# Branch hint, first score unit by halves, and a split last output piece in a soft-capped attention and token/channel mixer

## The chip, the core and the metric

The kernel runs on one core of one Trainium2 chip. The metric is the device time of one execution in microseconds (us). The kernel before took 591.39 us (median of 3 runs, 590.9 to 591.47).

## The reference, cut to what matters

```python
batch, heads, seq, head_dim = 4, 12, 448, 64          # attention
scores = tanh((q @ k.T) / sqrt(64) / cap) * cap       # soft cap
attn = exp(scores - max); attn /= attn.sum(-1) + 1e-9
x = heads_side_by_side(attn @ v)                      # 4 x 448 x 768

h = relu(x.T @ w_tok1) @ w_tok2                       # token mixing, 448 -> 256 -> 448
u = x + h.T
out = u + relu(u @ w_ch1) @ w_ch2                     # channel mixing, 768 -> 1536 -> 768
```

All inputs and the output are float32.

## The kernel before, in words

The work has three parts. The **attention** works on pairs of heads (two heads of 64 rows fill the 128 partitions) and on blocks of 128 keys: a score unit (`qk_unit`, line 349) is a matmul of a key block with all 448 queries for both heads. ScalarE then takes its tanh (`tanh_unit`, line 384) and its exp (line 394), and a `pv` unit multiplies the result with v. The first score units use plain float32 operands straight from the load (line 363); each such matmul call is issued to TensorE as two weight loads and two matmuls. Later units use operands split in a high and a low part. **Token mixing** is filled into the gaps of the attention. The **channel mixing** runs in six groups of 256 hidden channels; for each group and each of the 4 batches a `ch1` stage (line 834, 36 matmuls of 448 columns) makes the hidden values and a `ch2` stage (line 864, six output pieces of 6 matmuls) multiplies them back. `add_out` (line 883) lets VectorE add each piece to u and, in the last group, sends the sum to the output with one DMA per piece from SP's queue. The very last piece is added and sent in two halves of 224 columns, the first from SP's queue and the second from ScalarE's.

The first instructions are written by hand. `load_pair` (line 305) brings q and k of the first head pair in three DMAs: q on SP's queue (line 308), the first 128 keys on ScalarE's queue (line 309), and, after the small `cap` (line 310), the other keys on SP's queue (line 311). Behind them SP issues the second pair, v, the third pair and v twice more (lines 313 and 334). Two warm-up matmuls (line 742) keep TensorE busy meanwhile. After that a planner written in the kernel (`Plan`, line 87) simulates the engines with fixed costs and decides the order in which jobs are emitted; its costs are not touched by the change.

Near the end there is a **branch**. The fast way of computing holds only where `cap` is at most 40, so `big` is loaded from `mag` (line 1024) and compared (line 1025). All engines take this branch. The arm that runs here holds the last `ch1`, the `ch2` that was pending and the last `ch2` (lines 1028 to 1030). The other arm, `general()` (line 996), recomputes everything slowly and is never run with these inputs; with `preferred_fallthrough_block=False` its instructions lie directly behind the branch in the program, and the arm that runs lies behind them, about 9,970 TensorE instructions further on. `general()` calls `ch2` too (line 1021), with the same last piece. A branch hint for this branch is asked for at line 958, after `ch1` of the last group's third batch; the call names no engine.

Of the kernel before, what the change touches and what calls it, by code (L numbers as in the profile page):

```python
# [11 lines left out]
AF = mybir.ActivationFunctionType  # L12
ALU = mybir.AluOpType
PSUM = bass.MemoryType.PSUM

P = 128
B, H, S, D = 4, 12, 448, 64
C = H * D
NC = C // P
# [8 lines left out]
GF = 2  # L28
NG = FF // (GF * P)
# [4 lines left out]
FREE = 40.0  # L34
EPS = 1e-9
WARM = 2
WHOLE = S + NF * P
TERMS = ((0, 0), (1, 0), (0, 1))

SWITCH = {("pv", "qk"): 200, ("qk", "bg"): 195, ("bg", "pv"): 147, ("qk", "pv"): 143, ("bg", "qk"): 199}  # L40
DRAIN = 250
# [45 lines left out]
class Plan:  # L87
# [27 lines left out]
    def job(self, engine, cost, took, emit, *deps, slack=0.0, key=None):  # L115
        deps += (self.pe if self.at is None else self.at,)
        j = Job(cost, took if engine in ("sp", "pool") else took + SIGNAL, emit, deps, slack)
        self.jobs[engine].append(j)
        if key is not None:
            self.done[key] = j  # L120
        return j
# [48 lines left out]
def tile_softcap_mixer(ctx, tc, qk, v, cap, w1, w2, wc1, wc2, out):  # L170
    nc = tc.nc
# [11 lines left out]
    tsc = const.tile([P, 1], F32, name="tsc")  # L183
# [3 lines left out]
    u = [const.tile([P, NC, S], F32, name=f"u{b}") for b in range(B)]  # L187
# [11 lines left out]
    plan = Plan()  # L199
    job, done = plan.job, plan.done  # L200
# [6 lines left out]
    def room(n):  # L207
        return rings[n].room
# [85 lines left out]
    def half(i, j):  # L294
        return slice((i ^ j) * D, ((i ^ j) + 1) * D)
# [4 lines left out]
    def fine(b, p):  # L300
        return (b, p) >= FINE
# [3 lines left out]
    def load_pair(b, p):  # L305
        raw = pi.tile([P, 2, S], F32, tag="qkraw", name="qkraw", bufs=3)
        if b == 0 and p == 0:
            nc.sync.dma_start(raw[:, 0], qk[b, p, :, 0])
            nc.scalar.dma_start(raw[:, 1, :P], qk[b, p, :, 1, :P])
            nc.sync.dma_start(cap_sb, cap)  # L310
            nc.sync.dma_start(raw[:, 1, P:], qk[b, p, :, 1, P:])
        else:
            nc.sync.dma_start(raw, qk[b, p])
        raws[b, p] = raw
        holds["raw", b, p] = rings["raw"].take(NK)
        if not fine(b, p):
            return
        hi, lo = (pi.tile([P, WHOLE], F32R, tag=f"qk{x}", name=f"qk{x}", bufs=3) for x in ("hi", "lo"))
        parts[b, p] = hi, lo
        both = raw.rearrange("p x s -> p (x s)")[:, :WHOLE]  # L320
        near_first = len(parted) < INSIDE
        parted.append((b, p))

        def high():
            nc.gpsimd.dma_start(hi, both if near_first else qk[b, p].rearrange("p x s -> p (x s)")[:, :WHOLE])

        def low():
            nc.vector.tensor_tensor(lo, both, hi, op=ALU.subtract)

        job("pool", 560, 4 * P * WHOLE, high, *([("raw", b, p)] if near_first else []), slack=1500.0, key=("hi", b, p))  # L330
        job("dve", 1020, 1040, low, ("hi", b, p), ("raw", b, p), slack=LATER, key=("lo", b, p))
# [5 lines left out]
    def fetch(b, p):  # L337
        job("sp", 373, 8 * P * S, lambda: load_pair(b, p), room("raw"), slack=1500.0, key=("raw", b, p))
# [10 lines left out]
    def qk_unit(b, p, c):  # L349
        ps = ps_a.tile([P, 2, 512], F32, tag="a", name="ps_qk")  # L350
        hold = rings["a"].take(1)
        if c < NF and fine(b, p):
            two = parts[b, p]
            ks = slice(S + c * P, S + (c + 1) * P)
            for n, (x, y) in enumerate(TERMS):
                for j in range(2):
                    r = slice(j * D, (j + 1) * D)
                    nc.tensor.matmul(ps[:, j, :S], two[x][r, ks], two[y][r, :S], start=(n == 0), stop=(n == 2))  # L358
        elif c < NF:
            raw = raws[b, p]  # L360
            for j in range(2):
                r = slice(j * D, (j + 1) * D)
                nc.tensor.matmul(ps[:, j, :S], raw[r, 1, c * P:(c + 1) * P], raw[r, 0], start=True, stop=True)
        else:
            for i in range(2):
                raw = raws[b, p + i]
                for j in range(2):
                    r = slice(j * D, (j + 1) * D)
                    nc.tensor.matmul(
                        ps[half(i, j), i, :S], raw[r, 1, NF * P:S], raw[r, 0], start=True, stop=True  # L370
                    )
        t = plan.spend(612 if fine(b, p) and c < NF else 750, "qk")
        for i in range(2 if c == NF else 1):
            h = holds["raw", b, p + i]
            h.read(t)
            if len(h.by) == NK:
                raws.pop((b, p + i))
                parts.pop((b, p + i), None)
                n = pairs.index((b, p + i)) + 3
                if n < len(pairs):  # L380
                    fetch(*pairs[n])
        tanh = job("act", 891, 1009, lambda: tanh_unit(b, p, c, ps, hold, tanh), t + DRAIN, room("e"))

    def tanh_unit(b, p, c, ps, hold, tanh):
        e = pe.tile([P, 2, S], F32, tag="e", name="e", bufs=8)
        nc.scalar.activation(e, ps[:, :, :S], AF.Tanh, scale=tsc)  # L386
        hold.read(tanh)
        es[b, p, c] = e
        holds["e", b, p, c] = rings["e"].take(3 if c == NF else 2)
        job("act", 932, 1042, lambda: exp_unit(b, p, c), tanh.end - 190, slack=300.0, key=("exp", b, p, c))  # L390
# [349 lines left out]
    zeros = nc.const_aps.tensor(0.0, [P, HALF], F32)  # L740
    for _ in range(WARM):
        nc.tensor.matmul(idle[:, :HALF], zeros[:, :P], zeros, start=True, stop=True)
# [50 lines left out]
    while t < steps_in:  # L793
        n = 2 if PAIRED[0] <= t < PAIRED[1] else 1
# [33 lines left out]
    def await_key(key):  # L828
        await_time(lambda: plan.ready([key]))

    def await_weights(name, g, i):
        await_key(((name, g), i // DU * DU))
# [30 lines left out]

    def ch2(w, b, x, last, g=0):
        await_key(("g", g, b))
        for cc in range(NC):
            clear(lambda: rings["b"].room() is None and rings["c"].room() is None)
            n, tag = min((free_at(tag), tag) for tag in ("b", "c"))
            plan.pe = max(plan.pe, n)
            ps = (ps_b if tag == "b" else ps_c).tile([P, 512], F32, tag=tag, name="ps_o")  # L870
            hold = rings[tag].take(1)
            cs = slice(cc * P, (cc + 1) * P)
            n = 0
            for i in range(GF):
                await_weights("wc2", g, i * C + cc * P)
                for wi, gi in ((0, 0), (1, 0), (0, 1)):
                    nc.tensor.matmul(ps[:, :S], w[:, wi, i, cs], x[:, gi, i, :], start=(n == 0), stop=(n == 3 * GF - 1))  # L877
                    n += 1
            plan.spend(6 * 204)
            hold.read(job("dve", 530, 612, lambda cc=cc, ps=ps: add_out(b, cc, ps, last), plan.pe + DRAIN))  # L880
            fill()

    def add_out(b, cc, ps, last):
        end = last and b == B - 1 and cc == NC - 1
        for i, q in enumerate((nc.sync, nc.scalar) if end else (nc.sync,)):
            r = slice(i * S // 2, (i + 1) * S // 2) if end else slice(0, S)
            nc.vector.tensor_tensor(u[b][:, cc, r], u[b][:, cc, r], ps[:, r], op=ALU.add)  # L887
            if last:
                q.dma_start(out[b, :, cc, r], u[b][:, cc, r])

    def free_at(tag):
        t = rings[tag].room()
        return float("inf") if t is None else t
# [12 lines left out]
    def clear(more):  # L906
        while more():
            if not chunk():
                rest()
# [31 lines left out]
    w = w0  # L941
    for g in range(NG):
        if g + 1 < NG:
            nxt, steps = group_weights(
                g + 1, ([("tok",)], [("tok",)]) if g == 0 else ((), [("ch2", g - 1)]), slack=60000.0
            )
            for step in steps:
                step()
        if g == 0:
            pend = first_group(w)  # L950
            w = nxt
            continue
        for b in range(B):
            if g == NG - 1 and b == B - 1:
                break
            gt = ch1(w[0], b, g)
            if g == NG - 1 and b == B - 2:
                tc.mark_branch_hint_location("big", hint="LikelyTaken")
            ch2(*pend)
            if pend[1] == B - 1:  # L960
                done["ch2", pend[4]] = plan.pe
            pend = (w[1], b, gt, g == NG - 1, g)
        w = nxt
# [117 lines left out]
```

## Time and profile before

| | us |
|---|---|
| median of 3 runs | 591.39 |
| the profiled execution's own time | 589.29 |
| span of its instructions | 587.5 |
| TensorE busy (matmuls) | 579.7 |
| ScalarE busy | 255.5 |
| VectorE busy | 405.0 |

A row of a timeline has start, length, engine, line, operation, output and inputs, how many instructions it merges, and in brackets the idle time of the engine just before with what ended it. PE is TensorE's matmuls, PEld its weight loads; a q behind an engine's name (SPq, PEldq) is work of its instruction sequencer: DMA issues, branches, semaphores. "issue" is idle time in which the engine waited for nothing that the profile shows.

### The profile page before, as it was taken

Reading aid. Unit: us, or ns where it says so; the run is one execution under the profiler, and the core shown is the slowest. Engines: PE = TensorE matmul, PEld = TensorE weight load, DVE = VectorE, ACT = ScalarE, POOL = GpSimd, SP = SyncE. Lnnn points to the kernel's source line nnn. Section 1 sums busy time; section 2 is a strip of 40 time slices with the busy share of each in tenths; the row PEclk is TensorE's granted clock in tenths of the full one; section 3 lists DMA queues with packets and bytes.
Section 4 is the critical chain, followed back from the end, with each engine's and each line's share of the span. In section 5 each row is a group of like instructions: output and inputs, shape, how many; then the busy total and the mean of one; then the engine's idle time right before and its main releaser. Section 6 shows DMA issues by size and latency. Waiting matters only on the chain.

```text
span 587.5 us, 7994 instructions
## 1 busy us (share of the span) xinstructions
PE 579.7 (99%) x3102; PEld 449.5 (77%) x3102; DVE 405.0 (69%) x681; ACT 255.5 (43%) x330; POOL 9.2 (2%) x23
## 2 busy tenths in 40 slices
PE   8999999999999999999999999999999999999997
PEld 2233445545647899999999999999999999999986
DVE  2999999999999987479895568356835653333324
ACT  7999999899796433142430212021202110000000
POOL 0000100001000000000000000000000000000000
PEclk9999999999999999999999999999999999999999
DMA  7544684667521140003342032003200200000224
GB/s 243 183 148 137 193 260 161 207 222 227 180 80 38 38 134 6 1 1 98 117 144 73 0 108 79 29 0 108 77 32 1 71 1 0 1 0 32 94 84 172
DMA packets 26779, 55.51 MB, mean 94 GB/s; under 512 B 7024, under 2 KB 16752, under 8 KB 26736
## 3 DMA queue, kind: packets, MB, share of 16 engines
q1 hardware_dynamic: 24288, 48.37, 25.6%
q0 software_dynamic: 2160, 6.39, 3.9%
q8 instruction: 26, 0.43, 0.3%
q10 hardware_dynamic: 288, 0.18, 0.1%
q14 instruction: 17, 0.14, 0.1%
HBM read 47.97 MB, written 5.59 MB: 91 GB/s over the span
## 4 chain that ended last, share of the span: by engine, by line
PE 63%; DMA 1%; DVE 1%; issue 1%; SPq 0%; ACT 0%; DVEq 0%
PE ps_o L877 30%; PE ps_g L845 28%; PE ps_u L615 2%; PE ps_h L592 2%; DMA rs<-sums 1%; PE ps_t L564 1%; DMA rb<-rs 0%; DVE uhl L716 0%; DVE u L621 0%; DVE g L858 0%; DVE wz L246 0%; DVE wc L260 0%; SPq L544 0%; ACT uhl L713 0%; DVE u L887 0%
## 5 line engine op out<-in xcount | busy, mean ns | idle before, releaser
L877 PE MATMUL ps_o<-g,wc 128*128 128x448 f32 x864 | 181.7, 367 | 0.0
L877 PEld LDWEIGHTS ps_o<-g,wc 128*128 128x128 f32 x864 | 161.8, 188 | 14.4
L845 PE MATMUL ps_g<-uhl,wc 128*128 128x448 f32 x648 | 137.6, 367 | 0.0
L845 PEld LDWEIGHTS ps_g<-uhl,wc 128*128 128x128 f32 x648 | 121.1, 188 | 10.5
L887 DVE TENSOR_TENSOR u<-u,ps_o 128x448 f32<-128x448 f32 (+1 forms) x145 | 87.5, 615 | 45.3 <-PE ps_o L877 45.0
L386 ACT ACTIVATE e<-ps_qk,tsc 128x896 f32<-128x896 f32 x84 | 81.4, 1026 | 8.2 <-PE ps_qk L358 3.5
L394 ACT ACTIVATE e<-e,near 128x896 f32<-128x896 f32 x84 | 84.7, 1064 | 0.0
L855 ACT ACTIVATE g<-ps_g 128x896 fp32r<-128x896 f32 x24 | 22.1, 920 | 140.9 <-PE ps_g L845 140.8
L858 DVE SCALAR_TENSOR_TENSOR g<-ps_g,g 128x896 fp32r<-128x896 f32 x24 | 26.1, 1089 | 74.7 <-ACT g L855 74.7
L434 PE MATMUL ps_pv<-e,vn 128*64 128x448 f32 x288 | 60.5, 549 | 0.9 <-ACT e L394 0.9
L256 ACT ACTIVATE wc<-wz 128x512 fp32r<-128x512 f32 x36 | 22.8, 633 | 82.2 <-PE ps_g L845 36.0
L845 PE MATMUL ps_g<-last_u,wc 128*128 128x448 f32 x216 | 45.8, 368 | 1.2 <-PE ps_o L877 0.7
L845 PEld LDWEIGHTS ps_g<-last_u,wc 128*128 128x128 f32 x216 | 40.5, 188 | 5.7 <-issue 1.7
L434 PEld LDWEIGHTS ps_pv<-e,vn 128*64 128x64 f32 x288 | 18.0, 136 | 34.7 <-issue 24.2
L233 ACT ACTIVATE wz<-wraw 128x512 f32<-128x512 f32 x36 | 24.0, 670 | 37.8 <-DVE wc L260 17.4
L260 DVE TENSOR_TENSOR wc<-wz,wc 128x512 fp32r<-128x512 f32 x36 | 24.8, 688 | 21.2 <-ACT wc L256 19.9
L592 PE MATMUL ps_h<-wc,last_u 128*128 128x384 f32 x176 | 33.0, 336 | 0.0
L615 PE MATMUL ps_u<-last_u,wc 128*128 128x448 f32 x144 | 32.9, 371 | 0.0
L592 PEld LDWEIGHTS ps_h<-wc,last_u 128*128 128x128 f32 x176 | 30.8, 188 | 1.0 <-issue 0.6
L473 DVE TENSOR_TENSOR acc<-acc,e 64x448 f32<-64x448 f32 x48 | 29.7, 619 | 1.4
L615 PEld LDWEIGHTS ps_u<-last_u,wc 128*128 128x128 f32 x144 | 26.4, 188 | 5.2 <-issue 1.6
L456 DVE TENSOR_TENSOR acc<-e 128x896 f32<-128x896 f32 x24 | 26.0, 1084 | 6.1 <-ACT e L394 5.8
(59 smaller groups left out, 466.1 us busy)
## 6 DMA issues: line engine op xcount, KB each, us to landing
wraw<-in_wc SPq DMA_DIRECT2D x36, 512.0 KB, 3.5
qkraw<-in_qk SPq DMA_DIRECT2D x23, 448.0 KB, 4.0
vn<-in_v SPq DMA_DIRECT2D x24, 224.0 KB, 3.0
rb<-rs SPq DMA_DIRECT2D x48, 112.0 KB, 3.0
out_t<-u SPq DMA_DIRECT2D x23, 224.0 KB, 1.9
qkhi<-in_qk POOLq DMA_DIRECT2D x12, 416.0 KB, 4.0
qkhi<-qkraw POOLq DMA_DIRECT2D x3, 416.0 KB, 3.3
wraw<-in_w SPq DMA_DIRECT2D x2, 512.0 KB, 5.7
```

The costliest lines, as they stand in the source:

```text
L260: nc.vector.tensor_tensor(lo, bits(held["z"]), hi, op=ALU.subtract)
L386: nc.scalar.activation(e, ps[:, :, :S], AF.Tanh, scale=tsc)
L394: nc.scalar.activation(e, e, AF.Exp, scale=near)
L434: nc.tensor.matmul(o, vn[x % 3][:, j * NF + c], es[b, p, c][:, j], start=first, stop=last)
L456: nc.vector.tensor_tensor(accs[b, q][0][:, i], es[b, p, 0], es[b, p, 1], op=ALU.add)
L473: nc.vector.tensor_tensor(t, t, es[b, p - i, NF][r, i], op=ALU.add)
L592: nc.tensor.matmul(ps[:, :HALF], w, x, start=(n == 0), stop=(n == len(mm) - 1))
L615: nc.tensor.matmul(ps[:, :S], h1[:, hi, t, cs], w2s[:, wi, t, :], start=(n == 0), stop=(n == 3 * NT - 1))
L845: nc.tensor.matmul(ps[:, i, :S], w[:, wi, cc, fs], uhl[b][:, ui, cc, :], start=(n == 0), stop=(n == 3 * NC - 1))
L858: nc.vector.scalar_tensor_tensor(x[:, 1], ps[:, :, :S], 0.0, x[:, 0], op0=ALU.max, op1=ALU.subtract)
L877: nc.tensor.matmul(ps[:, :S], w[:, wi, i, cs], x[:, gi, i, :], start=(n == 0), stop=(n == 3 * GF - 1))
L887: nc.vector.tensor_tensor(u[b][:, cc, r], u[b][:, cc, r], ps[:, r], op=ALU.add)
```

## The change

The hint is asked for after `ch1` of the last group's first batch instead of the third. The first score unit is computed in two halves of 224 query columns, with q's load split the same way (the second half of q goes behind `cap`, ahead of the rest of k), and its tanh is two instructions. The last output piece is computed as two pieces, columns 0 to 335 and 336 to 447, each with its own six matmuls, its own add and its own DMA; the halves of 224 columns are gone.

```diff
+TAIL = 336
     def load_pair(b, p):
         if b == 0 and p == 0:
-            nc.sync.dma_start(raw[:, 0], qk[b, p, :, 0])
+            nc.sync.dma_start(raw[:, 0, :S // 2], qk[b, p, :, 0, :S // 2])
             nc.scalar.dma_start(raw[:, 1, :P], qk[b, p, :, 1, :P])
             nc.sync.dma_start(cap_sb, cap)
+            nc.sync.dma_start(raw[:, 0, S // 2:], qk[b, p, :, 0, S // 2:])
             nc.sync.dma_start(raw[:, 1, P:], qk[b, p, :, 1, P:])
...
-            for j in range(2):
-                r = slice(j * D, (j + 1) * D)
-                nc.tensor.matmul(ps[:, j, :S], raw[r, 1, c * P:(c + 1) * P], raw[r, 0], start=True, stop=True)
+            for n in columns(b, p, c):
+                for j in range(2):
+                    r = slice(j * D, (j + 1) * D)
+                    nc.tensor.matmul(ps[:, j, n], raw[r, 1, c * P:(c + 1) * P], raw[r, 0, n], start=True, stop=True)
...
+    def columns(b, p, c):
+        return [slice(0, S // 2), slice(S // 2, S)] if b == p == c == 0 else [slice(0, S)]
...
-        nc.scalar.activation(e, ps[:, :, :S], AF.Tanh, scale=tsc)
+        for n in columns(b, p, c):
+            nc.scalar.activation(e[:, :, n], ps[:, :, n], AF.Tanh, scale=tsc)
...
     def ch2(w, b, x, last, g=0):
-        for cc in range(NC):
+        pieces = [(cc, slice(0, S)) for cc in range(NC)]
+        if last and b == B - 1:
+            pieces[-1:] = [(NC - 1, slice(0, TAIL)), (NC - 1, slice(TAIL, S))]
+        for cc, r in pieces:
...
-                    nc.tensor.matmul(ps[:, :S], w[:, wi, i, cs], x[:, gi, i, :], start=(n == 0), stop=(n == 3 * GF - 1))
+                    nc.tensor.matmul(ps[:, r], w[:, wi, i, cs], x[:, gi, i, r], start=(n == 0), stop=(n == 3 * GF - 1))
...
-    def add_out(b, cc, ps, last):
-        end = last and b == B - 1 and cc == NC - 1
-        for i, q in enumerate((nc.sync, nc.scalar) if end else (nc.sync,)):
-            r = slice(i * S // 2, (i + 1) * S // 2) if end else slice(0, S)
-            nc.vector.tensor_tensor(u[b][:, cc, r], u[b][:, cc, r], ps[:, r], op=ALU.add)
-            if last:
-                q.dma_start(out[b, :, cc, r], u[b][:, cc, r])
+    def add_out(b, cc, r, ps, last):
+        nc.vector.tensor_tensor(u[b][:, cc, r], u[b][:, cc, r], ps[:, r], op=ALU.add)
+        if last:
+            (nc.scalar if r.start else nc.sync).dma_start(out[b, :, cc, r], u[b][:, cc, r])
...
             gt = ch1(w[0], b, g)
-            if g == NG - 1 and b == B - 2:
+            if g == NG - 1 and b == 0:
                 tc.mark_branch_hint_location("big", hint="LikelyTaken")
```

## Rows read from the trace of the kernel before

**Rows 1.** Windows: busy us (instructions) of each engine; then granted clock, DMA share, GB/s.
```profile
20.00:40.00 20.00, 20.00 (x114) 5.95 (x112) 19.55 (x35) 20.00 (x24) 0.30 (x1) 1.00 0.57 174
...
454.50:558.20 103.70, 103.70 (x508) 95.10 (x507) 41.62 (x67) 10.24 (x13) 0.00 (x0) 1.00 0.08 29
```
**Rows 2.** Chain that ended last, from 555 us (start, us, what).
```profile
560.45 0.69 issue
...
563.61 0.47 issue
...
569.39 14.74 PE ps_o L877 x72
```
**Rows 3.** The branch's line and the hint's line (duration ns min/median/max, start).
```profile
L1025 PEldq COMPARE_BRANCH  x1: 3732/3732/3732, 557.2 to 557.2; - x1
...
nothing on L958; most used: ['L877', 'L845', 'L434', 'L358', 'L592', 'L615', 'L363', 'L369', 'L564', 'L437', 'L485', 'L887', 'L386', 'L394', 'L215', 'L246', 'L233', 'L473', 'L517', 'L544', 'L554', 'L256', 'L530', 'L1076', 'L889']
```
**Rows 4.** Instruction fetches (packets, MB, share): 454.5 to 558.2, 558.2 to 559.7, 561.6 to 562.9.
```profile
q8 instruction: 4, 0.07, 0.2%
...
q8 instruction: 1, 0.02, 5.6%
...
q8 instruction: 1, 0.02, 5.2%
```
**Rows 5.** Timeline of weight loads behind the branch.
```profile
561.11 2.32 PEld L845 LDWEIGHTS ps_g<-last_u,wc 128*128 128x128 f32 x12 [1.06 <-issue]
564.08 4.93 PEld L845 LDWEIGHTS ps_g<-last_u,wc 128*128 128x128 f32 x24 [0.65 <-issue]
```
**Rows 6.** Line of the first score units (duration ns, first and last start).
```profile
L363 PE MATMUL ps_qk<-qkraw x108: 536/536/809, 3.9 to 61.6; 64*128 64x448 f32 x108
```
**Rows 7.** SP's queue at the start, timeline.
```profile
0.75 0.40 SPq L308 DMA_DIRECT2D qkraw<-in_qk  x1
...
1.68 0.43 SPq L311 DMA_DIRECT2D qkraw<-in_qk  x1
```
**Rows 8.** DMA issues at the start (KB each, us from issue to landing).
```profile
qkraw<-in_qk SPq DMA_DIRECT2D x1, 224.0 KB, 2.9
qkraw<-in_qk SPq DMA_DIRECT2D x1, 160.0 KB, 3.4
```
**Rows 9.** Timeline of weight loads and of ScalarE at the first units.
```profile
3.87 0.47 PEld L363 LDWEIGHTS ps_qk<-qkraw 64*128 64x128 f32 x4 [1.33 <-DMA qkraw<-in_qk]
5.13 0.30 PEld L363 LDWEIGHTS ps_qk<-qkraw 64*128 64x128 f32 x4 [0.80 <-DMA qkraw<-in_qk]
...
5.11 2.10 ACT L386 ACTIVATE e<-ps_qk,tsc 128x896 f32<-128x896 f32 x2 [2.44 <-PE ps_qk L363]
7.11 1.03 ACT L394 ACTIVATE e<-e,near 128x896 f32<-128x896 f32 x1
```
**Rows 10.** Timeline of the last add and the last DMA issue.
```profile
584.15 0.69 DVE L887 TENSOR_TENSOR u<-u,ps_o 128x224 f32<-128x224 f32 x2 [0.61 <-PE ps_o L877]
584.87 0.36 ACTq L889 DMA_DIRECT2D out_t<-u  x1
```
**Rows 11.** Lines with narrower matmuls, and the adds (duration ns min/median/max).
```profile
L592 PE MATMUL ps_h<-wc,last_u x176: 332/334/442, 71.0 to 253.1; 128*128 128x384 f32 x176
...
L564 PE MATMUL ps_t<-ident,u x96: 270/272/332, 42.2 to 242.0; 128*128 128x128 f32 x96
...
L887 DVE TENSOR_TENSOR u<-u,ps_o x145: 380/620/623, 224.3 to 584.5; 128x448 f32<-128x448 f32 x143, 128x224 f32<-128x224 f32 x2
```
**Rows 12.** Chain, longer stretches of those lines (start, us, what).
```profile
218.46 3.82 PE ps_h L592 x22
222.28 0.44 PE ps_t L564 x4
```
**Rows 13.** The output's DMAs, all and the two halves (KB, us to landing).
```profile
out_t<-u SPq DMA_DIRECT2D x23, 224.0 KB, 1.9
...
out_t<-u ACTq DMA_DIRECT2D x1, 112.0 KB, 1.7
```

More of the change, by code (lines that the diff above doesn't have):

```diff
@@ L876, in ch2 @@
                 for wi, gi in ((0, 0), (1, 0), (0, 1)):
-                    nc.tensor.matmul(ps[:, :S], w[:, wi, i, cs], x[:, gi, i, :], start=(n == 0), stop=(n == 3 * GF - 1))
+                    nc.tensor.matmul(ps[:, r], w[:, wi, i, cs], x[:, gi, i, r], start=(n == 0), stop=(n == 3 * GF - 1))
                     n += 1
             plan.spend(6 * 204)
-            hold.read(job("dve", 530, 612, lambda cc=cc, ps=ps: add_out(b, cc, ps, last), plan.pe + DRAIN))
+            hold.read(job("dve", 530, 612, lambda cc=cc, r=r, ps=ps: add_out(b, cc, r, ps, last), plan.pe + DRAIN))
             fill()
-    def add_out(b, cc, ps, last):
-        end = last and b == B - 1 and cc == NC - 1
-        for i, q in enumerate((nc.sync, nc.scalar) if end else (nc.sync,)):
-            r = slice(i * S // 2, (i + 1) * S // 2) if end else slice(0, S)
-            nc.vector.tensor_tensor(u[b][:, cc, r], u[b][:, cc, r], ps[:, r], op=ALU.add)
-            if last:
-                q.dma_start(out[b, :, cc, r], u[b][:, cc, r])
+    def add_out(b, cc, r, ps, last):
+        nc.vector.tensor_tensor(u[b][:, cc, r], u[b][:, cc, r], ps[:, r], op=ALU.add)
+        if last:
+            (nc.scalar if r.start else nc.sync).dma_start(out[b, :, cc, r], u[b][:, cc, r])
     def free_at(tag):
```

## Prediction

> **What bounds the kernel now.** I read the windows first. In the attention ScalarE is the full engine: busy 20.00 of 20.00 us, while TensorE's weight loads fill only 5.95. In the channel mixing it is TensorE: 103.70 of 103.70 us, with ScalarE at 10.24 [rows 1]. So time won or lost at the first tanh reaches the end only through ScalarE's queue, and in the channel mixing every nanosecond that TensorE stands still is paid. The chain that ended last shows where it stands still at the end: 0.69 us at 560.45, directly at the branch, and 0.47 us at 563.61, in the middle of a `ch1` stage whose operands had long been ready. Both are put down to "issue", a wait for nothing that the profile knows. From 564.08 on it runs without a gap, the last 72 matmuls in 14.74 us, 0.205 each [rows 2].
>
> The branch's line explains both. TensorE's sequencer, which runs ahead of the array, begins the branch at 557.2 and spends 3732 ns on it [rows 3]: until 560.97 no further instruction enters TensorE's queue. The array had work until 560.45, so 3.2 us of it are hidden and 0.69 (1.06 for the weight loads) are seen. The instruction fetches say what it waited for. Queue 8 made four fetches between 454.5 and 558.2 [rows 4], while TensorE ran 508 + 507 = 1015 instructions [rows 1]: one fetch per about 256 instructions, about 17 KB each. The next is in 558.2 to 559.7, after the branch had begun: the target was brought in only when the branch asked for it. One more follows in 561.6 to 562.9 [rows 4], and the second gap ends after it. Behind the branch 12 weight loads run, and then the loads stop for 0.65 us [rows 5]. One semaphore wait, 12 loads and 11 matmuls make 24 instructions: **the branch's target lies 24 instructions before the end of its fetched block**, and the next block, asked for only after the jump, comes 0.47 us too late.
>
> **Part 1, the hint, and what it would have to do.** No row of the trace stands on the hint's line [rows 3], though branches, register loads and semaphore waits of all engines are recorded. The call names no engine, and the program of the kernel before holds no hint instruction; the moved call names none either. I take that it adds nothing: 0 us. If it did work, the target would come early and both gaps would go, -1.16; that is rival 2.
>
> **A side effect: where the code comes to lie.** The change lengthens TensorE's program in two places ahead of the branch's target. The first score unit has four matmul calls instead of two; line 363 has 108 matmuls for 27 units of two calls [rows 6], so a call is two loads and two matmuls, and the two new calls are 8 instructions. `general()` lies between branch and target, and its `ch2` is split as well: 6 loads and 6 matmuls more, 12 instructions. The target moves 20 instructions on against the blocks of 256, from 24 before a block's end to 4: a semaphore wait, a load, a matmul, a load. The branch itself moves by 8 and is still not in the target's block, so it waits as before. TensorE then has one matmul instead of 11 to do while the second block is brought. If that block arrives when it does now, at 564.08, ten matmuls at 0.205 come after the gap instead of before it: **+2.05**. Bounds: if the second fetch is set off by reaching the block's end and not by the jump, it starts up to 0.65 us earlier (561.0 instead of about 561.65), +1.4. If coming to the end at once costs a fresh request like the branch's own (it began its fetch about 1 us after 557.2, against about 0.7 between the jump's end and the second), +2.4. The near row is the second fetch as it is, so I take 2.05. Nothing covers it: in this stretch TensorE is the chain.
>
> The Trainium skill ("Runtime: NRT & Kernel Launch", section "Instruction fetch mechanics") says that running over the end of a 16 KiB instruction block is mostly hidden, since the next one is fetched while the current one runs. By that sentence the term of 2.05 would be 0; the trace agrees with it for the straight stages, where no gap is seen, and not behind the branch, where the 0.47 stands. It is rival 1.
>
> **Part 2, the start.** Today q's 224 KB are issued at 0.75 and land 2.9 later, the rest of k is issued at 1.68 and lands 3.4 later, at 5.08 [rows 7, 8]. The first unit's loads start at 3.87 and the second unit's at 5.13, both on a DMA; the two tanhs run from 5.11, 2.10 us together, and the first exp starts at 7.11 [rows 9]. After the change q's second half takes the slot at 1.68, so k's rest is issued at 2.15, 0.47 later, and so is every load that SP issues behind it. The first half tanh comes early, at perhaps 4.6, and ScalarE does both halves before 5.9. But the second tanh waits for the second unit, and that for k's rest, at 5.08 + 0.47 = 5.55. ScalarE's queue is in order, so the early half waits in front of it: the second unit shifts by about **+0.45**. Bounds: the bytes ahead of k's rest are the same as before, so if the transfers themselves were the limit it lands at 5.1 again and the shift is -0.1 (the 2.10 for two tanhs hold about 0.1 of waiting); if the narrower rows of q (896 bytes) move no faster than its full ones did, another 0.35 comes on top, +0.8. ScalarE being full, I let two thirds reach the end: +0.3, range -0.1 to +0.8. The later loads (pair 2, v) are asked for in the same order and needed some microseconds after; their 0.47 is hidden behind the tanhs and exps of the first units.
>
> **Part 3, the end.** Six matmuls of 448 columns take 6 x 0.205 = 1.23 now. For 384 columns 22 take 3.82, 0.174 each, and for 128 columns 4 take 0.44, 0.11 each [rows 11, 12]; between 384 and 448 a column costs 0.48 ns. 336 columns: 0.150, six are 0.90. 112 columns: by that slope 0.042, but the near row is the 128-column one, whose weight loads set the pace: 0.11, six are 0.66. Together 1.56, TensorE ends 0.33 later. The first piece's add (about 0.50) and its DMA lie beside the second piece's matmuls and land first. Then the add of 112 columns: 380 ns at 224 columns and 620 at 448 [rows 11] give 0.26, against 0.69 for today's two halves [rows 10]. The last issue moves by 0.33 + 0.26 - 0.69 = -0.10. The last DMA carries 56 KB instead of 112; 224 KB take 1.9 and 112 take 1.7 [rows 13], so 1.6: -0.1. Sum **-0.2**. Bounds: 112 columns at 0.042 give -0.6; at the full 0.205 each, +0.37.
>
> The Trainium skill ("DMA: Bandwidth & Descriptors", section "Specifications") asks for pieces of at least 512 bytes, and 112 columns are 448 bytes per partition. If that doubles the 0.1 us that I give these 56 KB to move, the estimate for this part is -0.1 instead of -0.2; no row here shows a store that narrow.
>
> **Sum.** 2.05 + 0.3 - 0.2 + 0 = +2.15, say +2.1. The profiled execution took 589.29 (span 587.5 and 1.8 around it), so it would be 591.4; the median of the runs stands 2.1 above it at 591.39, and the same step gives **593.5**.
>
> **Rivals.** (1) *The crossing is hidden, or falls elsewhere.* The block's end does not come 4 instructions behind the target: either the 0.47 had another cause, or the number of semaphore waits in `general()` changes by four or more with the planner's state and the target slips into a fresh block. Then the 2.05 is 0 (or -0.47), and the rest leaves +0.1 (or -0.4): 591.5 (591.0), not slower. It decides from the fourth extra instruction on. For it: the other arm is planned anew after a changed piece; against it: a semaphore wait is added only where an instruction has two things to wait for, and the edits add none of that sort. 0.18. (2) *The hint takes effect.* Issued before TensorE enters the branch's block at about 531 it brings the target in time, both gaps go: -1.16 + 0.1, 590.3. Against it: the line without a row. 0.06. (3) *The longer pause slows the array.* The first matmuls of line 363 took 809 ns against a median of 536 [rows 6]; if after 2.7 us of standing still some ten or fifteen matmuls ran at half pace, 0.2 us each, another 2 to 3 us come on top: 596. For it only that first row; against it, matmuls after the 0.69 us gap ran at full pace. 0.04. My forecast, 0.72, has its own range: 1.4 - 0.1 - 0.4 to 2.4 + 0.7 + 0.2, that is 592.4 to 594.6.
>
> The range over the cases reaches down to rival 1 and leaves out the -0.4 variant's low side, rivals 2 and 3: 591.1 to 594.6. A measurement of this kernel tells about 0.2% (1.2 us) from no change. Slower by more than that: nearly all of the forecast and rival 3, 0.73. Within: rival 1, half of rival 2 and the forecast's low end, 0.22. Faster: the other half of rival 2 and what I do not see, 0.05.
>
> **What would show it.** TensorE's branch at line 1025 still near 3.7 us; two weight loads instead of 12 behind the branch, then an issue gap of 2 us or more, ending about 3 us after the jump; no row on the hint's line. At the start, a first tanh near 4.6 and the second unit's loads near 5.6. At the end, six matmuls at 0.15 and six near 0.11, and the last issue 0.1 us nearer to them. Wrong if the stretch behind the branch shows no longer gap, or if the branch takes well under 3 us.

## The result, and the profile after

The changed kernel takes 595.17 us (median of six runs, 593.5 to 597.63), the kernel before 591.38 in six runs beside them: a ratio of 1.0072, 95% [1.006, 1.0083], or +4.3 us [3.5, 4.9] (the two medians alone differ by 3.8). I had forecast 593.5 (591.1 to 594.6): slower, as it came, but by half as much. The profiled execution of after took 594.71 (span 592.8), 0.5 below its median, while that of before lay 2.1 below its own; so the two spans differ by 5.3 us, and about one of these is no work of the change.

The chain of after that ended last (start, us, what), against [rows 2]:

```profile
561.59 0.69 issue
562.28 0.44 PE ps_g L852
562.73 2.85 issue
565.58 8.92 PE ps_g L852 x35
574.50 15.04 PE ps_o L887 x78
589.53 0.02 issue
589.56 0.27 DVE u L894
```

The line numbers are those of the changed kernel: its line 852 is line 845 of before, 887 is 877, 894 is 887 and 1032 is 1025. The first gap is the one of before, 0.69. The second is 2.85 us instead of 0.47 and stands behind one matmul instead of 11. Then there is something that has no counterpart in before: the 36 matmuls of this `ch1` take 0.44 + 8.92 = 9.36 us, where before took 7.79 (2.47 + 5.32):

```profile
561.14 2.47 PE ps_g L845 x11
564.08 5.32 PE ps_g L845 x25
```

The windows of after say why (length; busy us and instructions of PE, PEld, DVE, ACT, POOL; granted clock; DMA share, GB/s):

```profile
562.00:565.00 3.00, 0.44 (x1) 0.19 (x1) 0.23 (x1) 0.00 (x0) 0.00 (x0) 1.00 0.43 153
565.00:567.00 2.00, 1.42 (x5) 1.30 (x6) 0.00 (x0) 0.00 (x0) 0.00 (x0) 0.80 0.06 18
567.00:569.00 2.00, 2.00 (x7) 1.73 (x7) 0.00 (x0) 0.00 (x0) 0.00 (x0) 0.50 0.00 0
569.00:571.00 2.00, 2.00 (x10) 1.85 (x9) 0.00 (x0) 0.00 (x0) 0.00 (x0) 0.85 0.00 0
571.00:573.00 2.00, 2.00 (x12) 1.85 (x11) 0.00 (x0) 0.00 (x0) 0.00 (x0) 1.00 0.00 0
```

Behind the long pause the granted clock falls to 0.50, the lower of the engine's two levels (1.2 instead of 2.4 GHz), and in those 2 us 7 matmuls run instead of the usual 11 or 12. PE is "busy" 2.00 of 2.00 there: the busy share alone would have hidden it. Before has 1.00 in every one of these windows, as its own row for 567 to 569 shows:

```profile
567.00:569.00 2.00, 2.00 (x11) 1.83 (x10) 0.00 (x0) 0.00 (x0) 0.00 (x0) 1.00 0.00 0
```

The branch, and the weight loads behind it, against [rows 3, 5]:

```profile
L1032 PEldq COMPARE_BRANCH  x1: 3729/3729/3729, 558.4 to 558.4; - x1
```
```profile
562.25 0.19 PEld L852 LDWEIGHTS ps_g<-last_u,wc 128*128 128x128 f32 x1 [1.06 <-issue]
565.58 4.49 PEld L852 LDWEIGHTS ps_g<-last_u,wc 128*128 128x128 f32 x15 [3.14 <-issue]
```

One load runs instead of 12, then the loads stop for 3.14 us instead of 0.65. The hint's new line has no row, as its old one had none.

The instruction fetch in 562.8 to 564.3, against the last of [rows 4]:

```profile
q8 instruction: 1, 0.02, 5.7%
```

It took 5.7% of 16 engines' 1.5 us, some 1.36 us, where that of before took 5.2% of 16 times 1.3, 1.08.

The start, ScalarE and the weight loads of after, against [rows 9], and the end, against [rows 10]:

```profile
5.73 2.18 ACT L393 ACTIVATE e<-ps_qk,tsc 128x448 f32<-128x448 f32 x3 [3.05 <-PE ps_qk L366]
7.80 1.03 ACT L401 ACTIVATE e<-e,near 128x896 f32<-128x896 f32 x1
```
```profile
3.62 0.51 PEld L366 LDWEIGHTS ps_qk<-qkraw 64*128 64x128 f32 x4 [1.08 <-DMA qkraw<-in_qk]
4.56 1.25 PEld L366 LDWEIGHTS ps_qk<-qkraw 64*128 64x128 f32 x8 [0.44 <-DMA qkraw<-in_qk]
```
```profile
588.95 0.88 DVE L894 TENSOR_TENSOR u<-u,ps_o 128x336 f32<-128x336 f32 x2 [0.31 <-PE ps_o L887]
589.86 0.35 ACTq L896 DMA_DIRECT2D out_t<-u  x1
```

The first half's loads run at 3.62, but no tanh starts before 5.73; the first exp begins 0.69 later than in before. At the end, 78 matmuls take 15.04 instead of 14.74 for 72, and from TensorE's end to the end of the span it is 592.8 - 589.53 = 3.27 us instead of 587.5 - 584.13 = 3.37.

So the 5.3 us between the two profiles are: +1.14 that had gathered by the end of the stage ahead of the gaps (560.45 to 561.59), +2.38 for the second gap, +1.57 for the slower matmuls, +0.30 for the narrower ones, -0.10 behind them. Which of these belong to the change, and what sets them off, the runs below tell.

### The profile page after: what moved, and what is told of

Its sections match the earlier page's. It is cut to its first block, busy times and chain, and to the rows that moved or that the text cites. A ratio compares the mean times of both kernels' runs of the same rounds, so it can differ in the third digit from the quotient of the medians.

```text
span 592.8 us, 8018 instructions
## 1 busy us (share of the span) xinstructions
PE 583.4 (98%) x3112; PEld 452.4 (76%) x3112; DVE 405.1 (68%) x681; ACT 255.7 (43%) x331; POOL 9.1 (2%) x23
## 4 chain that ended last, share of the span: by engine, by line
PE 90%; ACT 6%; issue 2%; DVE 2%; DVEq 0%; ACTq 0%
PE ps_g L852 30%; PE ps_o L887 30%; PE ps_pv L441 7%; PE ps_qk L360 5%; PE ps_h L599 5%; PE ps_u L622 5%; ACT e L393 3%; ACT e L401 2%; PE ps_t L571 2%; PE ps_s L492 2%; PE ps_pv L444 1%; PE ps_qk L372 1%; PE ps_qk L366 1%; PE idle L749 0%; DVE acc L470 0%
## 5 line engine op out<-in xcount | busy, mean ns | idle before, releaser
L887 PE MATMUL ps_o<-g,wc 128*128 128x448 f32 (+1 forms) x870 | 181.9, 365 | 0.0
L393 ACT ACTIVATE e<-ps_qk,tsc 128x896 f32<-128x896 f32 (+1 forms) x85 | 81.5, 1016 | 9.4 <-PE ps_qk L366 3.9
L852 PE MATMUL ps_g<-last_u,wc 128*128 128x448 f32 x216 | 47.4, 377 | 3.6 <-issue 2.9
L852 PEld LDWEIGHTS ps_g<-last_u,wc 128*128 128x128 f32 x216 | 41.8, 194 | 8.3 <-issue 4.2
```

The costliest lines, as they stand in the source:

```text
L393: nc.scalar.activation(e[:, :, n], ps[:, :, n], AF.Tanh, scale=tsc)
L852: nc.tensor.matmul(ps[:, i, :S], w[:, wi, cc, fs], uhl[b][:, ui, cc, :], start=(n == 0), stop=(n == 3 * NC - 1))
L887: nc.tensor.matmul(ps[:, r], w[:, wi, i, cs], x[:, gi, i, r], start=(n == 0), stop=(n == 3 * GF - 1))
```

## Experiments

Each ratio is to runs of the kernel before on the same chip; the medians of before in them lie between 591.2 and 591.7 us, so kernels of different chips are compared by their ratios. "n left" is how many instructions TensorE's target has to the end of its block, counted in its program from the 24 of before; after has 3, not 4, since a semaphore wait came in ahead of the branch. Where there is a second gap the traces bear the counts out: a semaphore wait, and the weight loads and matmuls that run ahead of the gap (5 and 5 in pad6, 8 and 8 in pad3).

### The place of the code alone

Nothing that is executed differs; only `general()`, which isn't run, grows, by ten transposes in `pad10`, 14 in `pad14`, and four on top of the changed kernel in `after4`. A transpose is two instructions, and one more comes with the block: 21 in `pad10`, 29 in `pad14`, 9 in `after4`.

```diff
     def general():
+        pad = ps_c.tile([P, 512], F32, tag="c", name="ps_pad")
+        for _ in range(10):
+            nc.tensor.transpose(pad[:, :P], ident, ident)
```

**pad10** (3 left):

> The kernel before, and ten transposes more in the arm that isn't run: nothing that is executed differs, but TensorE's target moves 21 instructions down, to the place that it has in the changed kernel (3 left in its block). Theory of the layout with the clock: the second gap behind the branch is 2.85 us instead of 0.47, the clock falls after it and 35 matmuls take about 1.8 us longer; 591.4 + 2.4 + 1.8 = 595.5 us, chain gaps 0.69 and 2.85, a granted clock near 0.64 in the stretch 3 to 6 us behind the second gap. Rival, layout without the clock (the fall came from the later start): 593.8 us, clock 1.00 behind the gap. Rival, the executed edits (start by halves, last piece) cost it all: 591.4 us.

Measured: 595.94 us, ratio 1.0059 [1.0041, 1.0078]. Its chain, and three of its windows:

```profile
562.06 1.17 issue
563.24 0.44 PE ps_g L845
563.67 3.30 issue
566.98 9.67 PE ps_g L845 x35
```
```profile
565.00:567.00 2.00, 0.02 (x1) 0.02 (x1) 0.00 (x0) 0.00 (x0) 0.00 (x0) 0.56 0.05 11
567.00:569.00 2.00, 2.00 (x5) 1.80 (x6) 0.00 (x0) 0.00 (x0) 0.00 (x0) 0.50 0.05 12
569.00:571.00 2.00, 2.00 (x7) 1.77 (x6) 0.00 (x0) 0.00 (x0) 0.00 (x0) 0.50 0.00 0
```

The kernel before, with its code moved and nothing else, is as slow as the changed one within the intervals: gap, fall of the clock and all. Here the clock is already down before the gap is over. Its last 72 matmuls take 14.73, as before.

**pad14** (251 left) and **after4** (250 left):

> The kernel before, and fourteen transposes more in the arm that isn't run, so that TensorE's target stands at the head of a block (251 instructions left). Theory of the layout: the second gap of 0.47 us goes, the first of 0.69 us stays; 590.9 us. Rival, the second gap is the wait for the block of the target itself and not for the one behind it: 591.4 us with both gaps as before.

> The changed kernel, and four transposes more in the arm that isn't run, so that the target has 250 instructions left in its block. Theory of the layout with the clock: the second gap goes (2.85 us) and with it the fall of the clock (1.8 us); 595.2 - 4.6 = 590.6 us, up to 591.2 if the loss at the start stays whole. Rival, the start by halves and the narrower last matmuls cost the time: 593 to 595 us, with the gap gone from the chain and the end as late.

Measured: 590.33 us, ratio 0.9977 [0.9965, 0.999], and 590.38 us, ratio 0.9976 [0.9961, 0.9992]. The chain of pad14, then that of after4:

```profile
561.84 1.22 issue
563.06 7.54 PE ps_g L845 x36
570.60 14.65 PE ps_o L877 x72
```
```profile
561.74 0.76 issue
562.50 7.68 PE ps_g L852 x36
570.17 15.04 PE ps_o L887 x78
```

The second gap is gone from both and the 36 matmuls run through. With the target near the head of its block, the changed kernel is as fast as the kernel before in the same place, and both are faster than before: within the intervals (about 0.9 us) all that the changed kernel loses, it loses by where its code lies. After against after4, the same executed work, is 595.17 against 590.38.

### How the loss goes with the place

**pad6** (11 left) and **pad3** (17 left):

> The kernel before and six transposes in the arm that isn't run: 11 instructions left, between the 24 of before and the 3 of the changed kernel. The layout gives a second gap in between, 2.9 us less the 1.2 us that the first ten instructions take, about 1.7 us (+1.2). If the clock falls after a pause of that length too: 591.4 + 1.2 + 1.8 = 594.4 us and a granted clock under 1 behind it; if only the longer pause brings the fall: 592.6 us and 1.00.

> The kernel before and three transposes in the arm that isn't run: 17 instructions left, between the 24 of before (gap 0.47 us, clock 1.00) and 11 (2.32 us, clock down to 0.50 behind it). By the layout the gap is about 1.2 to 1.7 us (+0.7 to +1.2). If a pause of that length brings the fall of the clock too: 591.3 + 1.0 + 1.8 = 594.1 us; if it stays at 1.00: 592.3 us.

Measured: 594.41 us, ratio 1.0065 [1.0048, 1.0082], and 592.35 us, ratio 1.0014 [1.0002, 1.0027]. Chain and one window of pad6, then of pad3:

```profile
562.90 1.25 PE ps_g L845 x5
564.15 2.32 issue
566.47 8.12 PE ps_g L845 x31
```
```profile
567.00:569.00 2.00, 2.00 (x7) 1.81 (x6) 0.00 (x0) 0.00 (x0) 0.00 (x0) 0.50 0.03 8
```
```profile
562.58 1.86 PE ps_g L845 x8
564.44 1.71 issue
566.15 5.94 PE ps_g L845 x28
```
```profile
567.00:569.00 2.00, 2.00 (x12) 1.85 (x11) 0.00 (x0) 0.00 (x0) 0.00 (x0) 1.00 0.04 8
```

| left | kernel | second gap, us | 36 matmuls, us | lowest clock behind it | ratio to before |
|---|---|---|---|---|---|
| 251 | pad14 | none | 7.54 | 1.00 | 0.9977 |
| 24 | before | 0.47 | 7.79 | 1.00 | 1 |
| 17 | pad3 | 1.71 | 7.80 | 1.00 | 1.0014 |
| 11 | pad6 | 2.32 | 9.37 | 0.50 | 1.0065 |
| 3 | after | 2.85 | 9.36 | 0.50 | 1.0072 |
| 3 | pad10 | 3.30 | 10.11 | 0.50 | 1.0059 |

The gap grows as the instructions that cover the fetch become fewer, but not by their number alone. The fetch of the second block, on queue 8, began 0.59 us behind the restart of the array in before, pad3, after and pad10 (1.05 in pad6). It took 1.08, 1.68, 1.36 and 1.89 us there (1.18 in pad6), and in all five the array went on about 1.3 us after it had ended: before's 0.47 goes with the shortest of these fetches.

Behind 1.71 us the clock stayed at 1.00 in pad3's profile, behind 2.32 us it fell in pad6's. By the ratios the kernel loses 0.8 us from 24 to 17 left and 3.0 more from 17 to 11, though the gap grows by only 0.6 there; pad6, after and pad10 can't be told apart. The length of the pause alone may not decide: the mean granted clock was 1.000 in ten of pad3's 12 runs and 0.997 in two, which took 593.87 and 593.63, the longest of the twelve. All runs of after, pad6 and pad10 had 0.993 to 0.997.

### The two executed parts alone

`start14` is before with the start by halves, `tail14` before with the last piece in 336 and 112 (and the hint at its new place, which emits nothing), both with the fourteen transposes of pad14.

> The kernel before with the start by halves alone (q's load, score, tanh of the first unit), and fourteen transposes in the arm that isn't run, so that the target has 242 instructions left in its block. Against the kernel before with the same fourteen transposes (590.33 us): if the start by halves costs what I forecast (+0.3) 590.6 us; if it costs the 0.7 us by which the second unit's tanh lay later in the changed kernel's profile, 591.0; rival, the shift is the spread of the first loads and not the edit's: 590.3.

> The kernel before with the last output piece in 336 and 112 columns alone (and the hint's place, which emits nothing), and fourteen transposes in the arm that isn't run; 239 instructions left in the target's block. Forecast of the tail -0.2: 590.1 us against 590.33; rival, the six matmuls more on the path (15.04 us for 78 instead of 14.7 for 72) cost more than the smaller last add and store give back: 590.6 us.

Measured: 590.58 us, ratio 0.999 [0.9981, 0.9999], and 590.13 us, ratio 0.9983 [0.9973, 0.9994], against pad14's 0.9977. The differences to pad14 (+0.0013 and +0.0006) are no larger than the intervals, so in the runs neither part alone can be told from nothing; after4 has both and the same ratio as pad14. The traces tell more. The last DMA issue of pad14 and that of start14:

```profile
585.99 0.35 ACTq L889 DMA_DIRECT2D out_t<-u  x1
586.55 0.36 ACTq L895 DMA_DIRECT2D out_t<-u  x1
```

From there to the end of the span it is 588.6 - 585.99 = 2.6 us in pad14, but 589.6 - 586.55 = 3.1 in start14, though the same store lands 1.7 us after its issue in both. At the end SyncE waits for the semaphores one after another, some 0.06 us each. In the 13 kernels without the halves the last store's semaphore is the last of this row; in the seven with them, which issue one DMA more at the start, seven waits still follow: **+0.4 us**. The new last piece for itself, tail14 against pad14, has 78 matmuls in 14.97 us instead of 72 in 14.65, +0.32, and 587.7 - 584.84 = 2.86 us behind them instead of 588.6 - 585.25 = 3.35: together -0.17.

### A hint that is issued

The call names no engine. With TensorE named, one instruction is emitted. In `named_tail` and `named_all` the last piece in 336 and 112 is there too, in `named_after` the whole change; `named_all` names all five engines, the others TensorE alone. `named_pad10` has the ten transposes of pad10.

```diff
-                tc.mark_branch_hint_location("big", hint="LikelyTaken")
+                tc.mark_branch_hint_location("big", hint="LikelyTaken", engines=[engines.PE])
```

> The kernel before, with TensorE named in the branch hint, so that an instruction for it is really issued there (one instruction more; the target has 23 left in its block). If the hint fetches the target ahead, the gap of 0.69 us behind the branch goes, and part of the 3.73 us of the branch itself may go: 590.7 us, down to 588 if the branch's time is mostly the fetch. Rival, the hint changes nothing on the path: 591.4 us.

> The kernel before with TensorE named in the branch hint and ten transposes in the arm that isn't run: 2 instructions left in the target's block. If the hint brings only the target's own block, the next one is still fetched after the branch: a gap near 2.9 us and the fall of the clock remain, and only the first 0.69 us goes, 595 us. Rival, the block behind is on its way before the branch ends (589.09 us with 23 left had no gap of either kind): a gap under 1 us, no fall, 589 to 590 us.

> The kernel before with the last output piece in 336 and 112 columns and TensorE named in the branch hint, nothing padded (11 instructions left). With the hint no gap behind the branch whatever the place (as with 23 and 2 left): 589.06 - 0.2 = 588.9 us, no fall of the clock. Rival, the hint only helped in places of luck: 594 us as with 11 left and no hint.

> As the run with TensorE named in the hint and the last piece in 336 and 112 columns, but all five engines named. If only TensorE's branch is on the path: 588.9 us, as with TensorE alone. Rival, the other engines' first fetches in the arm delay it as well (VectorE's split of the last g): 0.3 to 0.6 us less, 588.4 us; or five hints at the head cost some 0.1 us at the start: 589.0.

> The changed kernel whole, with TensorE named in its hint: 2 instructions left. If the layout and the clock are all that it lost: 589.06 (before, hint with TensorE, 2 left) + 0.25 (start) - 0.2 (last piece) = 589.1 us, 6 us under the changed kernel as it is. Rival, that something else in it costs time: over 590.5 us.

| kernel | left | us | ratio to before |
|---|---|---|---|
| named | 23 | 589.09 | 0.9959 [0.9943, 0.9974] |
| named_pad10 | 2 | 589.06 | 0.9964 [0.9949, 0.9978] |
| named_tail | 11 | 589.02 | 0.9956 [0.994, 0.9972] |
| named_all | 11 | 589.36 | 0.9959 [0.9942, 0.9975] |
| named_after | 2 | 590.29 | 0.9977 [0.9967, 0.9988] |

The hint's row and the branch's row in named, and the chain of named_pad10:

```profile
L1076 PEldq BRANCH_PREFETCH_HINT  x1: 50/50/50, 0.8 to 0.8; - x1
```
```profile
L1025 PEldq COMPARE_BRANCH  x1: 412/412/412, 558.1 to 558.1; - x1
```
```profile
554.42 7.36 PE ps_o L877 x36
561.78 7.44 PE ps_g L845 x36
569.22 14.74 PE ps_o L877 x72
```

The branch takes 0.41 us instead of 3.73, and both gaps are gone, with 2 left as with 23: the jump is over some 2.8 us before the array runs dry. No instruction fetch on queue 8 falls in 555 to 559 of named's trace, so its branch found the target there; with 23 left there was time for the next block too, if the fetch at 559.70 is its own. With 2 left this is not shown: the fetch at 559.72 in named_pad10 took 1.46 us, the array's first matmul behind the branch ran 0.6 us after it had ended and not 1.3, and so the block that was needed may have been there before. pad10 with this one instruction goes from 595.94 to 589.06. More engines than TensorE bring nothing that can be told. **named** and **named_tail** beat both kernels: 2.4 and 2.6 us under before, some 6 to 7 under the changed kernel.

named_after missed its forecast. Its chain keeps the first gap, and longer, but neither the second gap nor the slower matmuls:

```profile
562.24 1.35 issue
563.59 7.67 PE ps_g L852 x36
```

### What takes the hint's effect from the changed kernel

> The kernel before with TensorE named in the hint and the hint marked three stages sooner; nothing else. Theory of the code's place: the hint stands first in the program wherever it is marked, so this is the run with the hint at its old place over again: 589.1 us, TensorE's branch at 0.41 us, no gap. Rival, the sooner mark is what lost the hint's effect in the changed kernel with TensorE named (590.29 us, branch 4.33 us, gap 1.35 us): 590.3 us with both.

> The kernel before with the start by halves and TensorE named in the hint at its old place. The start adds nine TensorE instructions ahead of the branch, which then ends its block of 256 as in the changed kernel. Theory of the code's place: the hint misses, the branch takes about 4 us and a gap near 1.2 us stays, 590.3 us. Rival, the sooner mark lost the effect: 589.3 us here, branch 0.41 us, no gap.

> The kernel before with TensorE named in the hint and two matmuls of 8 columns more in the warm-up (eight instructions more ahead of the branch; nothing of the start or of the last piece changed). Theory of the code's place: the branch stands at the end of its block of 256 and the hint misses: branch about 4 us, gap near 1.2 us, 590.3 us. Rival, the executed edits of the start lost the effect: 589.1 us, branch 0.41 us, no gap.

> The changed kernel whole with TensorE named in its hint and two matmuls of 8 columns more in the warm-up, which move the branch eight instructions on, into the next block. Theory of the code's place: the hint works again, branch 0.41 us, no gap, 589.1 to 589.4 us. Rival, the sooner mark or the executed edits lost the effect: 590.3 us, branch about 4 us, a gap over 1 us.

`named_w2` and `named_after_w` add two matmuls of 8 columns to the warm-up; `named_odd` and `named_after_odd` add this one, on top of before and of the changed kernel:

```diff
+    nc.tensor.matmul(idle[:1, :1], near, ones[:, :1], start=True, stop=True)
```

> The kernel before with TensorE named in the hint and one tiny matmul of the start's constants in the warm-up, whose wait makes it five instructions: the branch stands at an even place of TensorE's program (6080). So far the hint worked with the branch at 6075 and 6083 and missed at 6084 and 6092, where the start by halves stood in the kernel too. If the even place loses the hint: branch about 4 us, a gap near 1 us, 590.3 us. Rival, the start by halves loses it: 589.1 us, branch 0.41 us, no gap.

> The changed kernel whole with TensorE named in the hint and the same tiny matmul: the branch stands at an odd place (6089). If the place's parity decides: branch 0.41 us, no gap, 589.2 us, which would make the whole change 2 us faster than the kernel before. Rival, the start by halves loses the hint: 590.4 us, branch about 4 us, a gap over 1 us.

| kernel | start by halves | branch is instruction | left | branch, us | first gap, us | ratio to before |
|---|---|---|---|---|---|---|
| named_hint | no | 6075 | 23 | 0.41 | none | 0.9965 |
| named_odd | no | 6080 | 18 | 0.41 | none | 0.9969 |
| named_w2 | no | 6083 | 15 | 0.40 | none | 0.9972 |
| named_start | yes | 6084 | 14 | 3.84 | 0.87 | 0.9988 |
| named_after | yes | 6084 | 2 | 4.33 | 1.35 | 0.9977 |
| named_after_odd | yes | 6089 | 253 | 4.30 | 1.26 | 0.9974 |
| named_after_w | yes | 6092 | 250 | 4.03 | 1.00 | 0.9992 |

The medians are 589.19, 589.12, 589.7, 590.45, 590.29, 589.81 and 590.83 us. The times alone do not part the two groups (0.9972 [0.9962, 0.9982] against 0.9974 [0.9962, 0.9985]); the branch and the first gap do. Where the branch waited, a fetch falls into it: queue 8 has one in 555 to 559 of named_start, none there in named.

The sooner mark is not the cause: named_hint is as named is, and its hint instruction runs at 0.8 us too, before the first warm-up matmul, wherever the call stands. So the change's first part moves nothing even with an engine named. Nor is it the parity of the branch's place (named_odd, named_after_odd). The start by halves and a place of 6084 or later still go together in all four that lost the effect; a kernel without the halves and the branch at 6084 or later would part them and was not run. The theory that the branch must not end its block got two of its four runs wrong (named_w2 kept the effect, named_after_w did not regain it). Half of the hint's work seems to be left: named_start (14 left) and named_after (2 left) have no second gap, which 17, 11 and 3 left without a hint had. In named_after_odd and named_after_w the target lies at the head of a block, where pad14 and after4 have no second gap without a hint either.

## Why the prediction was right in sign and wrong in size

**The hint, 0.** Right, for the reason given: no engine named, nothing emitted; the branch at 3729 ns against 3732.

**The place of the code, +2.05 (1.4 to 2.4).** Right, and its mechanism is shown by pad10, pad14 and after4. (One semaphore wait more, which I had argued against, left 3 instructions instead of 4.) It measured +2.38: from the restart to the end of the second gap it is 565.58 - 562.28 = 3.30 us, against 564.08 - 561.14 = 2.94 in before. That is the upper bound's size but not its reason, a fresh request at the block's end. The second fetch began 0.59 us behind the restart in both, as the middle value had it; it took 1.36 us instead of 1.08.

**The slower array, rival 3, chance 0.04.** This is the step that failed. I saw that some ten matmuls at half pace would cost 2 us and set it aside because "matmuls after the 0.69 us gap ran at full pace": I carried what a short pause does over to one four times as long. Behind 2.32 us and more the clock fell in every profile, and in after the 36 matmuls took 1.57 us longer. 2.38 + 1.57 is 3.95 of the measured 4.3; my forecast had the first term only. The rival's price, 2 to 3 us, was somewhat high here (2.3 in pad10), its chance far too low. The range was also narrower than its own parts: it took 0.7 and 0.2 at the top where they give 0.8 and 0.37. But with those it ends at 595.0, still under the measured 595.17.

**The start, +0.3.** About the size that the traces show, by luck: the place and the reasons were wrong. The rest of k was not late, and the early tanh that I expected near 4.6 did not come, since both halves' tanhs start only after the last matmul of the unit. The 0.69 us by which the first exp lay later in after is no price either: the second unit's tanh starts at 6.20 in before's profile, the earliest of all, at 6.20 to 7.92 (median 6.82) in the 13 profiles without halves, and at 6.58 to 7.13 (median 6.90) in the seven with them. The same goes for the +1.14 ahead of the gaps: pad10 and pad14, which execute what before does, end that stage at 562.06 and 561.84, later than after. What the halves do cost is the 0.4 us of waits at the program's end, which I had not in the sum.

**The end, -0.2 (-0.6 to +0.37).** Right by the traces, -0.17 in tail14, though the runs can't tell it from 0: 336 columns with 0.155 us and 112 with 0.112 each came as worked out, and so did the last add, 0.27, and the last store, which lands 1.6 us after its issue. That after's own profile gives +0.30 - 0.10 = +0.2 is the 0.4 us of the halves on top.

**Rival 1** (the crossing is hidden) is refuted. The Trainium skill ("Runtime: NRT & Kernel Launch", section "Instruction fetch mechanics") calls the crossing of a block mostly hidden; the traces agree in straight code and not behind the branch, up to 3.30 us in pad10. The same section of the Trainium skill warns that a taken branch to a block that isn't held stalls for its fetch; the 3729 ns agree with that. **Rival 2** (the hint takes effect) was false of this change, but its mechanism exists: named is 2.4 us faster, against the 1.16 that I gave it, which was worked out from a first gap of 0.69 where the other profiles without its effect have 0.76 to 1.35 (after alone has 0.69 too); the 36 matmuls, 7.44 us instead of 7.79, gain as well.

## What to carry to other kernels

Ahead of a taken branch on a full engine, ask where its target lies in the fetched blocks: padding code that isn't run, or a hint that names the engine, was worth more here than the edits that were meant to help, and a hint call without a row of its own in the trace did nothing. A pause on TensorE is priced with the granted clock behind it: look for the clock's row at the pause's length, not at a shorter one's. One DMA more at the start can cost time at the very end of the program, so compare the stretch behind the last store too. And a row of one execution is one draw: 0.7 us of the start and 1.1 us ahead of the branch were the spread between executions.

## What I had not expected of the hardware

Instructions that are never executed changed the time from 590.33 to 595.94 us (pad14, pad10). The hint instruction, run 557 us ahead of its branch, still held; it cut the branch from 3.73 to 0.41 us. And in named_start and named_after, where the branch waited in spite of it, the block behind the target was there without a gap; why one half of its effect went and the other stayed, no run shows. The start by halves, with its one DMA more, left seven waits of some 0.06 us each behind the last store.
